# Attention and residual MLP on one core: MLP vectors scaled as rows and split on GpSimd, first head's q and k in halves

## The chip, the cores and the metric

The kernel runs on one core of one Trainium2 chip. The core has a matrix engine (TensorE, PE in the profile, with its weight loads as PEld), a vector engine (VectorE, DVE), a scalar engine (ScalarE, ACT), a general engine (GpSimd, POOL), an engine that mostly starts transfers (SyncE, SP), and 16 DMA engines. Each engine works through its own instructions in order and waits on semaphores for the others. The metric is the device time of one execution in microseconds (us).

## The reference

Block-sparse attention over 4 batches of 8 heads, 768 tokens and 64 dimensions, with a mask made of blocks of 32 tokens (neighbours, the first and the last block, and three drawn blocks for each row of blocks), then a residual MLP over 512 columns.

```python
scores = np.where(mask, scale * q @ k.T, -1e9)
x = softmax(scores) @ v                       # heads side by side: 4 x 768 x 512
a1 = alpha1 * x + beta1
tok = np.einsum('ts,bsd->btd', w_tok, a1)
u = x + lam * tok
a2 = alpha2 * u + beta2
ch = np.maximum(a2 @ w_ch1, 0.0) @ w_ch2
return (u + lam * ch).astype(np.float32)
```

`lam`, `alpha1` and `beta1` are vectors of 512. The product with `lam` is folded into other factors: `alpha1` and `beta1` are multiplied by it before they are used (tok comes out scaled), and `w_ch2` is multiplied by it in place (L453).

## The kernel before

**Tiling.** Heads are taken in pairs: 16 pairs `i`, four to a batch. Tokens are laid out as 6 slots of 128 (`NT = 6`). A unit is one pair, one half of its queries (`c`, 384 of them) and one step `j` of six; each unit computes two 128-key tiles of transposed scores for one head (`emit_qk`, L324: two matmuls into an `sp` buffer), one exponential of 128x768 on ACT (L332), and, two units later, six value products (`emit_pv`, L345). There are 192 units, one to a slot `s` of the main loop (L735). For the first pair the units are ordered so that steps 0 to 2 (the first head) of both query halves come first.

**Mask.** Each key tile carries 24 rows more (`kText[n][64:88]`) with the mask for the key's block, and the queries carry 24 indicator rows (`indq`), so that the mask is added by the score matmul. `mbs` (24x24) is worked out by DVE from `sampi` and `ms` (L195 to L210), spread into `kText[0]` in three parts of 256 columns (`emit_mask_part`, three copies each, L230), and copied to the other three buffers with `emit_mask_rows` (L236, on DVE).

**Start.** The first pair is loaded in float32 through SP's and ACT's DMA queues (`load_first`, L148, one DMA of 192 KB for a head and a tensor), later pairs by POOL's queue with a cast to 16 bits (`emit_load`, L111). `emit_lay` (L126) copies q and k side by side into `qk`; `emit_tps` transposes the six slots on PE (L267), and DVE copies the results into `kText` (L273) and `qText` (L276). `emit_warm` (L260) puts filler matmuls on PE; `spare` in `emit_qk` (L316) does the same inside the units. A copy of one element of v (`gate`, L187) stands on POOL ahead of the loads of pair 1.

**Vectors.** The three MLP vectors are loaded as 12 rows of 128 (`vrows`, L166). `emit_parts` (L400 to L404, DVE) splits each row into three bfloat16 parts; `emit_bcast(n)` (L409) multiplies a selection matrix (`pick`, L172) with them on PE, which puts vector `n` on all 128 partitions; L418 copies lam out of PSUM, and L420 copies alpha1 and beta1, times lam. `emit_lam16` (L437) casts lam to bfloat16 for L453. `emit_a1pp` (L376, L377) on POOL uses the two products.

**MLP.** `emit_wtok_t` transposes w_tok (L468, copied by L469), `job_tok` multiplies it with `a1pp` (L485), `job_f1` and `job_f2` are the two dense products (L553, L572).

**Order.** It is written out by hand. `at(s, ...)` hangs functions into slot `s`; up to slot 54 they run at the slot's end, from slot `OPEN = 55` on before its value products, and there a queue of MLP jobs is poured in beside them. Engines execute in the order in which the program issues to them. Transfers on SP and ACT signal eight semaphores in rotation, so a DMA also waits for the one that used its semaphore before.

Of the kernel before, what the change touches and what calls it, by code (L numbers as in the profile page):

```python
# [20 lines left out]
S = 768  # L21
# [20 lines left out]
def kernel(  # L42
# [73 lines left out]
    def emit_lay(i, nm, w=slice(0, 2), copy=None):  # L116
        raw = raws[(i, nm)][:, w].rearrange("p w (o d) -> p w o d", d=D)
        if nm != "v" and i >= XP:
            dst = (qls if nm == "q" else kls)[i % 2][:, w, :, 0:D]
        elif nm == "v":  # L120
            dst = vexts[i % NVB][:, w, :, 0:D]
        else:
            if i not in qks:
                qks[i] = ap_.tile([P, 2, NT, 2, D], BF, name="qk", tag="qk", bufs=2)
            dst = qks[i][:, w, :, "qk".index(nm), :]
        (copy or nc.vector.tensor_copy)(out=dst, in_=raw)  # L126
# [20 lines left out]
    def load_first(nm, src, w, eng):  # L147
        eng.dma_start(  # L148
            raws[(0, nm)][:, w, :], src[0, w].rearrange("(p o) d -> p (o d)", o=NT)
        )  # L150

    load_first("q", q, 0, nc.sync)
    load_first("k", k, 0, nc.scalar)
# [3 lines left out]
    load_first("v", v, 0, nc.scalar)  # L157
    nc.sync.dma_start(qText[0][D : D + NBLK, :], indq_dr.ap())
    load_first("k", k, 1, nc.scalar)
# [4 lines left out]
    vrows = ptile([P, P], FP, "vrows")  # L164
    for n, src in enumerate((moe_lam, moe_alpha1, moe_beta1)):
# [19 lines left out]

    gate = ptile([P, 1], FP, "gate")
    nc.gpsimd.tensor_copy(out=gate[:], in_=raws[(0, "v")][:, 0, 0:1])  # L187
# [4 lines left out]
    emit_lay(0, "q", slice(0, 1))  # L192
    emit_lay(0, "k", slice(0, 1), nc.scalar.copy)
    rndf = ptile([P, NR], FP, "rndf")
    nc.vector.tensor_copy(out=rndf[0:NBLK, :], in_=sampi[0:NBLK, 0 : 2 * NR : 2])  # L195
    mbm = ptile([P, NBLK], FP, "mbm")
# [67 lines left out]
    def emit_tps(i, w):  # L264
        tps = mm_tile((P, NT, P), BF)
        for o in range(NT):
            nc.tensor.transpose(tps[:, o, :], qks[i][:, w, o], identb[:])  # L267
# [3 lines left out]
        qa = 0  # L271
# [108 lines left out]
    vbc = ptile([P, 3, DM], FP, "vbc")  # L380
    lam_bc, a1_bc, b1_bc = (vbc[:, n, :] for n in range(3))
# [16 lines left out]
    def emit_parts():  # L398
        r = slice(0, 12)
        nc.vector.tensor_copy(out=parts[r], in_=vrows[r])  # L400
        nc.vector.tensor_sub(out=rest[r], in0=vrows[r], in1=parts[r])
        nc.vector.tensor_copy(out=part[r], in_=rest[r])
        nc.vector.tensor_copy(out=parts[32:44], in_=rest[r])
        nc.vector.tensor_sub(out=parts[64:76], in0=rest[r], in1=part[r])  # L404

    def emit_bcast(n):
# [28 lines left out]

    def emit_lam16():
        nc.vector.tensor_copy(out=lam_bcb[:], in_=lam_bc)  # L437
# [237 lines left out]

    for s, n in ((0, 1), (1, 2), (2, 1)):
# [136 lines left out]
```

## Time and profile before

| | |
|---|---|
| median of 3 runs | 324.46 us (324.38 to 324.64) |
| time of the profiled execution | 324.88 us |
| span of the profiled execution | 323.1 us |
| PE busy | 315.6 us, 98% of the span |
| ACT busy | 223.2 us, 69% |
| DVE busy | 140.0 us, 43% |
| POOL busy | 99.0 us, 31% |
| exponentials (L332) | 192 of 901 ns |
| first dense products (L553) | 512 matmuls of 325 ns |
| first score matmul | at 6.19 us |
| first exponential | at 7.03 us |
| first matmul of L553 | at 57.68 us |

The span runs from the first instruction to the last; the time of a run also holds what lies around it (1.78 us for the profiled execution). A line of an engine's timeline gives the start, the busy time, the engine, the line and operation, what it writes and reads, and in square brackets how long the engine stood idle before it and who released it. An entry with x8 stands for eight instructions merged. Busy times of matmuls hold a drain that overlaps the next one.

### The profile page before, as it was taken

Reading aid. Unit: us, or ns where it says so; the run is one execution under the profiler, and the core shown is the slowest. Engines: PE = TensorE matmul, PEld = TensorE weight load, DVE = VectorE, ACT = ScalarE, POOL = GpSimd, SP = SyncE. Lnnn points to the kernel's source line nnn. Section 1 sums busy time; section 2 is a strip of 40 time slices with the busy share of each in tenths; the row PEclk is TensorE's granted clock in tenths of the full one; section 3 lists DMA queues with packets and bytes.
Section 4 is the critical chain, followed back from the end, with each engine's and each line's share of the span. In section 5 each row is a group of like instructions: output and inputs, shape, how many; then the busy total and the mean of one; then the engine's idle time right before and its main releaser. Section 6 shows DMA issues by size and latency. Waiting matters only on the chain.

```text
span 323.1 us, 7663 instructions
## 1 busy us (share of the span) xinstructions
PE 315.6 (98%) x3216; PEld 205.7 (64%) x3216; DVE 140.0 (43%) x289; ACT 223.2 (69%) x328; POOL 99.0 (31%) x128
## 2 busy tenths in 40 slices
PE   8889999999999999999999999999999999999996
PEld 3667878667675766676665756676665756555543
DVE  4889988557343345331534444242332434000011
ACT  4889998998878776878768675678877740553310
POOL 7566746443434411132525402142222200000000
PEclk9999999999999999999999999999999999999999
DMA  6999996969392976091665966097430011000012
GB/s 168 197 191 164 143 156 110 165 114 140 57 177 54 169 120 131 32 172 27 127 103 96 138 106 128 34 155 74 108 52 32 15 46 65 32 34 32 32 43 89
DMA packets 61898, 32.56 MB, mean 101 GB/s; under 512 B 42000, under 2 KB 58756, under 8 KB 61736
## 3 DMA queue, kind: packets, MB, share of 16 engines
q0 software_dynamic: 16608, 14.22, 31.2%
q1 hardware_dynamic: 44680, 17.23, 25.2%
q10 hardware_dynamic: 576, 0.62, 0.7%
q8 instruction: 25, 0.41, 0.5%
q14 instruction: 9, 0.07, 0.1%
HBM read 29.97 MB, written 6.29 MB: 112 GB/s over the span
## 4 chain that ended last, share of the span: by engine, by line
PE 90%; DVE 7%; POOL 1%; issue 1%; ACT 1%; DVEq 0%; POOLq 0%
PE mm L553 26%; PE mm L572 25%; PE sp L324 16%; PE mm L485 10%; PE op L345 9%; PE op L260 1%; PE mm L592 1%; DVE qTs L276 1%; DVE wtokT L469 1%; DVE kTs L273 1%; PE mm L267 1%; DVE qk L126 1%; DVE x_sb L362 1%; POOL a1pp L376 1%; POOL a1pp L377 1%
## 5 line engine op out<-in xcount | busy, mean ns | idle before, releaser
L332 ACT ACTIVATE eT<-sp,expb 128x768 f16<-128x768 f32 x192 | 170.4, 901 | 47.3 <-PE sp L324 44.6
L553 PE MATMUL mm<-uT,w1b 128*128 128x384 bf16 x512 | 100.1, 325 | 0.0
L324 PE MATMUL sp<-qTs,kTs 88*128 88x384 bf16 x384 | 95.5, 326 | 0.9 <-ACT eT L332 0.5
L572 PE MATMUL mm<-w2b,hts 128*128 128x512 bf16 x368 | 92.3, 379 | 0.0
L560 ACT ACTIVATE hts<-mm 128x384 bf16<-128x384 f32 x128 | 61.8, 488 | 35.4 <-PE mm L553 35.0
L376 POOL TENSOR_TENSOR a1pp<-x_sb,vbc 128x384 bf16<-128x384 f32 x28 | 28.3, 1009 | 150.7 <-DVE x_sb L362 150.7
L553 PEld LDWEIGHTS <-w1b 128*128 128x128 bf16 x512 | 49.3, 97 | 36.1 <-issue 0.9
L345 PEld LDWEIGHTS <-eT 128*128 128x128 f16 x1152 | 55.9, 97 | 21.9
L572 PEld LDWEIGHTS <-hts 128*128 128x128 bf16 x368 | 35.3, 97 | 33.9
L345 PE MATMUL op<-vext,eT 128*128 128x65 f16 x1008 | 53.8, 193 | 0.0
L581 DVE TENSOR_TENSOR ot<-x_sb,mm 128x512 f32<-128x512 f32 x23 | 15.8, 686 | 66.9 <-PE mm L572 66.9
L485 PE MATMUL mm<-a1pp,wtokT 128*128 128x128 bf16 x576 | 41.6, 219 | 0.9 <-DVE qTs L276 0.3
L485 PEld LDWEIGHTS <-wtokT 128*128 128x128 bf16 x576 | 35.6, 97 | 6.6 <-PE mm L345 0.4
L500 DVE TENSOR_TENSOR x_sb<-x_sb,mm 128x384 f32<-128x384 f32 x32 | 17.6, 550 | 49.3 <-PE mm L485 48.5
L324 PEld LDWEIGHTS <-kTs 88*128 88x128 bf16 x384 | 28.3, 98 | 6.9 <-issue 1.4
L377 POOL TENSOR_TENSOR a1pp<-a1pp,vbc 128x384 bf16<-128x384 bf16 x28 | 26.7, 952 | 2.2
L506 DVE CAST ubf<-x_sb 128x384 bf16<-128x384 f32 x32 | 17.7, 553 | 1.1
L360 DVE RECIPROCAL rcp<-op 128x6 f32<-128x6 f32 x28 | 5.3, 191 | 29.5 <-PE op L345 29.2
L362 DVE TENSOR_TENSOR x_sb<-op,rcp 128x384 f32<-128x384 f32 x28 | 15.6, 558 | 1.0
L539 DVE TENSOR_SCALAR uT<-uraw,ab2T 128x768 bf16<-128x768 bf16 x11 | 5.4, 493 | 16.8 <-DMA uraw<-ubf 16.8
L111 POOL DMA_DIRECT2D qr<-in_q_dram x15 | 11.4, 761 | 3.1 <-DVE qk L126 3.1
L111 POOL DMA_DIRECT2D kr<-in_k_dram x15 | 10.8, 721 | 0.9 <-DVE qk L126 0.9
(74 smaller groups left out, 147.4 us busy)
## 6 DMA issues: line engine op xcount, KB each, us to landing
out_dram<-ot SPq DMA_DIRECT2D x23, 256.0 KB
qr<-in_q_dram POOLq DMA_DIRECT2D x15, 192.0 KB, 4.6
kr<-in_k_dram POOLq DMA_DIRECT2D x15, 192.0 KB, 6.3
vr<-in_v_dram POOLq DMA_DIRECT2D x15, 192.0 KB, 6.8
w1b<-in_moe_w_ch_dram POOLq DMA_DIRECT2D x4, 512.0 KB, 6.4
w2b<-in_moe_w_ch_dram POOLq DMA_DIRECT2D x4, 512.0 KB, 6.7
hts<-in_moe_w_tok_dram POOLq DMA_DIRECT2D x1, 1152.0 KB, 11.2
kf<-in_k_dram ACTq DMA_DIRECT2D x2, 192.0 KB
```

The lines of the kernel that those rows point to most:

```text
L111: nc.gpsimd.dma_start(t[:], src[b, 2 * hp : 2 * hp + 2].rearrange("w (p o) d -> p w (o d)", o=NT))
L324: nc.tensor.matmul(sp[:, jj, 0:QC], kText[n][0 : D + NBLK, ts(2 * jp + jj, P)], qText[n][0 : D + NBLK, ts(c, QC)], start=True, stop=True,)
L332: nc.scalar.activation(eT[:], sp[:, :, 0:QC], AF.Exp, bias=expb[:], scale=SCALE)
L345: nc.tensor.matmul(op[:, w, o, :], eT[:, jj, ts(o, P)], vexts[i % NVB][:, w, 2 * jp + jj, :], start=(j == 0 and jj == 0 and o == 0), stop= ...
L362: nc.vector.tensor_tensor(out=x_sbs[b][:, ts(c, 3), cols].rearrange("p o (w d) -> p w o d", w=2), in0=op[:, :, :, 0:D], in1=rcp[:].unsquee ...
L376: eng.tensor_tensor(out=dst, in0=x_sbs[b][:, sl, cols], in1=bc[0], op=ALU.mult)
L377: eng.tensor_tensor(out=dst, in0=dst, in1=bc[1], op=ALU.add)
L485: nc.tensor.matmul(ps[:, o % 3, :], wtokT[:, os_, ts(o, P)], a1pps[i][:, os_, :], start=(os_ == 0 and o % 3 == 0), stop=(os_ == NT - 1 and ...
L506: nc.vector.tensor_copy(out=ubfs[i][:, sl, :], in_=x_sbs[b][:, sl, ts(hp, P)])
L553: nc.tensor.matmul(ps[:, 0:QC], w1b[:, dk, ts(n, P)], uTs[b][:, dk, ts(c, QC)], start=(dk == 0), stop=(dk == 3),)
L560: nc.scalar.activation(hts[(b, c)][:, n, :], ps[:, 0:QC], AF.Relu)
L572: nc.tensor.matmul(ps[:], ht[:, nk, ts(o % 3, P)], w2b[:, nk, :], start=(nk == 0), stop=(nk == NH - 1),)
```

## The change

Four things are changed.

1. The first head's q and k are loaded, cast and transposed in two halves of three slots. The first halves are both cast by DVE, of the second halves k by POOL and q by DVE. The first scores are issued between the two sets of transposes. One filler matmul less stands ahead of them. On the DMA queues, the second k half and the query indicators follow on ACT, and v and the second head's k move to SP. The gate copy is gone.
2. `lam` is loaded twice more, as rows beside alpha1 and beta1 (`lrows`, whose first four rows are ones). `emit_parts` runs on POOL, begins with the product of the rows, and is issued before the main loop, ahead of the load of w_tok. `emit_bcast` then only copies; alpha1 and beta1 go into slots 6 and 7, lam directly into its bfloat16 form in slot 61.
3. The mask rows of buffers 2 and 3 are copied by DMA from SP in slot 2 instead of by DVE in slots 9 and 11.
4. Some slots move: the casts and transposes of pair 3, one token job, and the two scalings of u.

```diff
-    load_first("q", q, 0, nc.sync)
-    load_first("k", k, 0, nc.scalar)
+    load_first("q", q, 0, nc.sync, 0)
+    load_first("k", k, 0, nc.scalar, 0)
     nc.sync.dma_start(sampi[0:NBLK, :], sampled_blocks.bitcast(I32))
     nc.scalar.dma_start(identb[:], ident_dr.ap())
     nc.sync.dma_start(ms[0:NBLK, :], ms_dr.ap())
-    load_first("v", v, 0, nc.scalar)
-    nc.sync.dma_start(qText[0][D : D + NBLK, :], indq_dr.ap())
-    load_first("k", k, 1, nc.scalar)
+    load_first("k", k, 0, nc.scalar, 1)
+    load_first("q", q, 0, nc.sync, 1)
+    nc.scalar.dma_start(qText[0][D : D + NBLK, :], indq_dr.ap())
+    load_first("v", v, 0, nc.sync)
+    load_first("k", k, 1, nc.sync)
     load_first("q", q, 1, nc.sync)
     load_first("v", v, 1, nc.sync)
...
+    lrows = ptile([P, P], FP, "lrows")
+    nc.gpsimd.memset(lrows[0:12], 1.0)
+    for n in (1, 2):
+        nc.sync.dma_start(
+            lrows[4 * n : 4 * n + 4, :], moe_lam.rearrange("(c d) -> c d", d=P)
+        )
...
-    gate = ptile([P, 1], FP, "gate")
-    nc.gpsimd.tensor_copy(out=gate[:], in_=raws[(0, "v")][:, 0, 0:1])
...
-    emit_lay(0, "q", slice(0, 1))
-    emit_lay(0, "k", slice(0, 1), nc.scalar.copy)
     rndf = ptile([P, NR], FP, "rndf")
     nc.vector.tensor_copy(out=rndf[0:NBLK, :], in_=sampi[0:NBLK, 0 : 2 * NR : 2])
+    for nm in "qk":
+        emit_lay(0, nm, slice(0, 1), o=slice(0, 3))
...
     cuts = [(0, 2 * P, QC), (2 * P, S, S)] if i == 0 else [(0, S, S)]
+    if part is not None:
+        cuts = [(0, QC, QC), (QC, S, S)][part : part + 1]
...
     def emit_parts():
-        r = slice(0, 12)
-        nc.vector.tensor_copy(out=parts[r], in_=vrows[r])
-        nc.vector.tensor_sub(out=rest[r], in0=vrows[r], in1=parts[r])
-        nc.vector.tensor_copy(out=part[r], in_=rest[r])
-        nc.vector.tensor_copy(out=parts[32:44], in_=rest[r])
-        nc.vector.tensor_sub(out=parts[64:76], in0=rest[r], in1=part[r])
+        r, eng = slice(0, 12), nc.gpsimd
+        eng.tensor_mul(out=vrows[r], in0=vrows[r], in1=lrows[r])
+        eng.tensor_copy(out=parts[r], in_=vrows[r])
+        eng.tensor_sub(out=rest[r], in0=vrows[r], in1=parts[r])
+        eng.tensor_copy(out=part[r], in_=rest[r])
+        eng.tensor_copy(out=parts[32:44], in_=rest[r])
+        eng.tensor_sub(out=parts[64:76], in0=rest[r], in1=part[r])
...
-        if n == 0:
-            nc.vector.tensor_copy(out=lam_bc, in_=ps[:])
-        else:
-            nc.vector.tensor_tensor(
-                out=vbc[:, n, :], in0=ps[:], in1=lam_bc, op=ALU.mult
-            )
+        nc.vector.tensor_copy(out=dst, in_=ps[:])
...
+    emit_mask_part(0, nc.scalar.copy)
+    emit_tps(0, 0, 0)
+    for nm, eng in (("k", nc.gpsimd), ("q", nc.vector)):
+        emit_lay(0, nm, slice(0, 1), eng.tensor_copy, o=slice(3, NT))
+    emit_mask_part(1, nc.scalar.copy)
+    emit_warm(1)
     emit_load(1)
-    emit_mask_part(0, nc.scalar.copy)
-    emit_mask_part(1, nc.scalar.copy)
-    emit_tps(0, 0)
-    emit_warm(2)
-    emit_mask_part(2, nc.vector.tensor_copy)
+    emit_parts()
     emit_wtk_load()
...
+    at(0, lambda: emit_tps(0, 0, 1))
+    at(0, lambda: emit_mask_part(2, nc.vector.tensor_copy))
...
-    at(4, emit_parts)
     at(5, lambda: emit_lay(0, "v", slice(1, 2)), emit_columns)
-    at(9, lambda: emit_mask_rows(2))
-    at(11, lambda: emit_mask_rows(3))
-    at(6, lambda: emit_bcast(0))
-    at(7, lambda: emit_bcast(1))
-    at(8, lambda: emit_bcast(2))
+    rows = slice(D, D + NBLK)
+    for i in (2, 3):
+        at(2, lambda i=i: nc.sync.dma_start(kText[i][rows, :], kText[0][rows, :]))
+    at(6, lambda: emit_bcast(1, a1_bc))
+    at(7, lambda: emit_bcast(2, b1_bc))
+    at(61, lambda: emit_bcast(0, lam_bcb[:]))
...
-    at(60, emit_lam16)
...
-        3: (20, 21, 28, 27, 32),
+        3: (23, 24, 29, 28, 32),
...
-    tok_at(0, (22, 24, 25, 26, 28, 29))
+    tok_at(0, (22, 24, 25, 26, 27, 29))
     at(30, lambda: emit_udma(0))
-    at(47, lambda: emit_uscale(0))
+    at(44, lambda: emit_uscale(0))
...
-    at(54, lambda: emit_uscale(1))
+    at(51, lambda: emit_uscale(1))
```

More of the change, by code (lines that the diff above doesn't have):

```diff
@@ L114, in emit_load, with emit_lay @@
             raws[(i, nm)] = t
-    def emit_lay(i, nm, w=slice(0, 2), copy=None):
-        raw = raws[(i, nm)][:, w].rearrange("p w (o d) -> p w o d", d=D)
+    def emit_lay(i, nm, w=slice(0, 2), copy=None, o=slice(0, NT)):
+        raw = raws[(i, nm)][:, w].rearrange("p w (o d) -> p w o d", d=D)[:, :, o]
         if nm != "v" and i >= XP:
@@ L124, in emit_lay @@
                 qks[i] = ap_.tile([P, 2, NT, 2, D], BF, name="qk", tag="qk", bufs=2)
-            dst = qks[i][:, w, :, "qk".index(nm), :]
+            dst = qks[i][:, w, o, "qk".index(nm), :]
         (copy or nc.vector.tensor_copy)(out=dst, in_=raw)
@@ L145, with load_first @@
     maskt = ptile([P, NT, NBLK], BF, "maskt")
-    def load_first(nm, src, w, eng):
+    def load_first(nm, src, w, eng, half=None):
+        cols = slice(0, NT * D) if half is None else ts(half, NT * D // 2)
         eng.dma_start(
-            raws[(0, nm)][:, w, :], src[0, w].rearrange("(p o) d -> p (o d)", o=NT)
-        )
-    load_first("q", q, 0, nc.sync)
-    load_first("k", k, 0, nc.scalar)
+            raws[(0, nm)][:, w, cols],
+            src[0, w].rearrange("(p o) d -> p (o d)", o=NT)[:, cols],
+        )
+    load_first("q", q, 0, nc.sync, 0)
+    load_first("k", k, 0, nc.scalar, 0)
     nc.sync.dma_start(sampi[0:NBLK, :], sampled_blocks.bitcast(I32))
@@ L262, with emit_tps @@
     emit_warm(8)
-    def emit_tps(i, w):
+    def emit_tps(i, w, part=None):
         tps = mm_tile((P, NT, P), BF)
-        for o in range(NT):
-            nc.tensor.transpose(tps[:, o, :], qks[i][:, w, o], identb[:])
         n = (2 * i + w) % NQB
         cuts = [(0, 2 * P, QC), (2 * P, S, S)] if i == 0 else [(0, S, S)]
-        qa = 0
+        if part is not None:
+            cuts = [(0, QC, QC), (QC, S, S)][part : part + 1]
+        qa = 0 if cuts[0][0] == 0 else QC
+        for o in range(qa // P, cuts[-1][2] // P):
+            nc.tensor.transpose(tps[:, o, :], qks[i][:, w, o], identb[:])
         for ka, kb, qb in cuts:
@@ L377, in emit_a1pp @@
         eng.tensor_tensor(out=dst, in0=dst, in1=bc[1], op=ALU.add)
-    vbc = ptile([P, 3, DM], FP, "vbc")
-    lam_bc, a1_bc, b1_bc = (vbc[:, n, :] for n in range(3))
+    vbc = ptile([P, 2, DM], FP, "vbc")
+    a1_bc, b1_bc = (vbc[:, n, :] for n in range(2))
     ab2 = ptile([P, P], FP, "ab2")
@@ L398, in emit_parts, with emit_bcast @@
     def emit_parts():
-        r = slice(0, 12)
-        nc.vector.tensor_copy(out=parts[r], in_=vrows[r])
-        nc.vector.tensor_sub(out=rest[r], in0=vrows[r], in1=parts[r])
-        nc.vector.tensor_copy(out=part[r], in_=rest[r])
-        nc.vector.tensor_copy(out=parts[32:44], in_=rest[r])
-        nc.vector.tensor_sub(out=parts[64:76], in0=rest[r], in1=part[r])
-    def emit_bcast(n):
+        r, eng = slice(0, 12), nc.gpsimd
[5 more added lines that the diff above has]
+        eng.tensor_sub(out=parts[64:76], in0=rest[r], in1=part[r])
+    def emit_bcast(n, dst):
         ps = mm_tile()
@@ L434, in emit_columns_use @@
         nc.vector.tensor_copy(out=ab2T[:], in_=tps[:])
-    def emit_lam16():
-        nc.vector.tensor_copy(out=lam_bcb[:], in_=lam_bc)
     def emit_w1_load(g):
```

## The prediction

> **What bounds the kernel now.** I read the page's shares first, then each engine in order of time, then what each wait waited for.
>
> ```profile
> span 323.1 us, 7663 instructions
> PE 315.6 (98%) x3216; PEld 205.7 (64%) x3216; DVE 140.0 (43%) x289; ACT 223.2 (69%) x328; POOL 99.0 (31%) x128
> ...
> ACT  4889998998878776878768675678877740553310
> ...
> L553 PE MATMUL mm<-uT,w1b 128*128 128x384 bf16 x512 | 100.1, 325 | 0.0
> ```
>
> TensorE (PE) is busy throughout, but before 58 us part of its work is filler (L260, L316). There ScalarE (ACT) is at 8 to 9 tenths: one exponential (L332) after another. From then on the dense products rule, and the first of them never waits (idle 0.0 on L553). So the program is an exp chain up to some 58 us and a fixed pile of PE work behind it: what the first part saves moves the end by as much. The exps, in order of time:
>
> ```profile
> 3.91 0.51 ACT L126 CAST qk<-kf 128x384 bf16<-128x384 f32 x1
> 5.30 1.08 ACT L230 COPY kTs<-mbs 24x96 bf16<-24x96 bf16 x6 [0.88 <-DVE mbs L210]
> 7.03 3.28 ACT L332 ACTIVATE eT<-sp,expb 128x768 f16<-128x768 f32 x4 [0.65 <-PE sp L324]
> 10.50 2.50 ACT L332 ACTIVATE eT<-sp,expb 128x768 f16<-128x768 f32 x3 [0.19 <-PE sp L324]
> 13.88 7.25 ACT L332 ACTIVATE eT<-sp,expb 128x768 f16<-128x768 f32 x8 [0.88 <-PE sp L324]
> 21.67 7.13 ACT L332 ACTIVATE eT<-sp,expb 128x768 f16<-128x768 f32 x8 [0.54 <-PE sp L324]
> 29.21 0.90 ACT L332 ACTIVATE eT<-sp,expb 128x768 f16<-128x768 f32 x1 [0.42 <-PE sp L324]
> 30.37 22.32 ACT L332 ACTIVATE eT<-sp,expb 128x768 f16<-128x768 f32 x26 [0.25 <-PE sp L324]
> 53.30 5.64 ACT L332 ACTIVATE eT<-sp,expb 128x768 f16<-128x768 f32 x6 [0.62 <-PE sp L324]
> ```
>
> Square brackets hold the idle time and who ended it. Besides the start at 7.03 us there are gaps of 0.88, 0.54, 0.42, 0.25 and 0.62. PE ends each, but was itself late for VectorE (DVE):
>
> ```profile
> 12.58 0.28 DVE L404 TENSOR_TENSOR parts<-rest,part 12x128 bf16<-12x128 f32 x1
> 13.01 0.38 PE L409 MATMUL mm<-parts,pick 96*128 96x128 bf16 x4 [0.64 <-DVE parts L404]
> ...
> 20.94 0.20 PE L433 MATMUL mm<-ident,ab 8*128 8x8 f32 x1 [0.81 <-DVE rcp L360]
> ...
> 28.28 0.51 PE L485 MATMUL mm<-a1pp,wtokT 128*128 128x128 bf16 x6 [0.30 <-DVE wtokT L469]
> ```
>
> **The start: halves.** Eight warm matmuls (L260) start at 1.19 and every 0.427 us, so PE is free at 4.60 whatever the data do; q and k land by 4.03 now (k's landing releases the ninth DMA, SP's second q, at 3.87). Half loads carry half the packets (1536 bytes take 65 ns, 256 take 18), so they land some 0.5 us sooner, and the DVE casts (half of L126's 0.36: 0.21 each) end near 4.1: under the warm matmuls. The gain is in the three transposes: six take from 4.58 to 5.22, 0.107 apart, so three save 0.32. The DVE copies of three slots, 0.35 each (the 64x384 row), end at 5.85; first scores 5.90 for 6.19, first exp near 6.74 for 7.03. ACT's mask copies (3 x 0.18) follow `mbs` at 4.9 and are ready at 5.45.
> It is given back at once. The second halves' transposes stand behind the first scores: 5.90 + 2 x 0.32 = 6.54 to 7.05; DVE's kT copy to 7.42; one score tile 0.17, drain 0.17 and 0.05 to ACT: second exp 7.83 (now 7.85). The last mask part (3 copies, 0.53) runs behind both copies, to 8.35, so third scores end at 8.88 and the third exp starts at 8.92 (now 8.67). PE has the fifth ready in time; it starts near 10.56 (now 10.50). This half of the change is worth nothing by itself.
>
> **Vectors on GpSimd (POOL).** DVE loses five small operations, 0.21+0.28+0.21+0.22+0.28 = 1.20 us, two mask-row copies (0.56+0.35, now SP DMAs) and one 0.69 us step of L420. POOL gets six operations on 12x128, which this trace does not show. A tensor-tensor lies between the 0.20 of a 128x128 memset and the 1.01 of L376 on 384 columns; interpolating from the 0.19 of the gate copy (one column), 0.45. A copy lies between 0.19 and the 0.43 of a 128x288 one: 0.30. With 0.07 between steps, 2.6 us (1.2 to 4.7). The kf half cast on POOL (0.19 to 0.5, I take 0.35) hides under the first scores, to 6.54.
> When can they start? SP waits before a ninth DMA for the first of the last eight:
>
> ```profile
> SPq L148 <- DMA kf<-in_k_dram: 1.4, 1, 1.4
> ...
> SPq L172 <- DMA qf<-in_q_dram: 0.4, 1, 0.4
> ```
>
> After the change v and second k are on SP too, and the three vrows stand behind them and two lrows: the beta row leaves when second k has landed (near 6.5) and its packets follow v's in the ring. In the landing records now, v's last part ends at 7.86 and beta at 8.57; I put beta at 9.0, parts done at 11.6. The picks (L172; the third landed 4.3 us after its issue at 7.38) come near 11.5. PE reaches the broadcast behind the value products of the fifth exp, at 12.40 with the rows above (now 12.36, when it begins to wait). So the wait goes, and exp 8 starts at 13.2 for 13.88: 0.65 gained. Behind the waiting POOL stand the w_tok load (issue 8.06 now, 11.7 then) and pair 2's loads. That is covered: the first w_tok packet moves in the trace at 11.5, behind pair 1, which now leaves 0.8 us sooner; 11.7 + 1.64 (pair 1's issue to first packet) + 5.4 (its bytes at 110 KB per half us) + 0.3 = 19.0 for 19.3 now, wanted at 20.6. Without that cover pair 2's q, wanted 1.3 us later, is late next.
> The queues otherwise: ACT still issues four DMAs ahead of its table load; its new fourth, the query indicator (L158), lands near 4.5 behind less data than now (5.30) and is wanted at 5.90. SP issues v, second k, q and v from 3.3 to 5.0, each released by one of the small first ones; DVE wants them at 8.4 to 11.6, and landing at 6 to 7.9 hides that. The mask-row DMAs wait on SP for DVE's last mask part (8.35), and the alpha2, beta2 loads behind them are wanted only at slot 14. The gate copy that held pair 1 back goes; the kf cast now stands in its place.
> In 21.67's gap DVE was late with pair 1's copies (its queue held a mask-row copy and the slowed 1.05 us vext copy): 0.35 of 0.54 goes. In 29.21's gap a pair 3 cast (0.92) stood ahead of the last wtokT copy; it moves three slots down: 0.3 of 0.42. The other two gaps I leave, between all gone (0.87) and doubled; the casts and scales shifted there move DVE work no PE row names.
>
> **Late cost.** The lam broadcast moves from slot 6 to 61, where PE is the bound: 4 x 0.055 = 0.22, and up to 0.3 more for a PSUM buffer held by a 0.68 copy; I take 0.3. The copy itself replaces a 1.13 us cast (L437) on a DVE that then idles.
>
> **Sum** against the execution's own 323.1 (its run took 324.88, 0.42 above the median): -0.65 - 0.35 - 0.30 + 0.30 = -1.0, a span of 322.1; on the median of 324.46, 323.5. Own range 322.5 to 323.9: all gaps gone (another 1.1) or half of the gain kept.
>
> **Rivals.** *The clock.* Rows:
>
> ```profile
> 6.19 0.80 PE L324 MATMUL sp<-qTs,kTs 88*128 88x384 bf16 x2
> 6.79 0.53 PE L260 MATMUL op<-warm 128*128 128x512 bf16 x1
> 7.15 0.49 PE L324 MATMUL sp<-qTs,kTs 88*128 88x384 bf16 x2
> ```
>
> A pair of score matmuls takes 0.80, then 0.49: PE doubles its pace near 7.1, while the granted clock reads 1.00 throughout. PE was idle 0.12 us in between; after the change it has one warm matmul less and idles from 5.35 to 5.90. If the idling put the doubling off by 2 to 3 us (the count so far took 5.9, from 1.19), the second to fourth scores and their warm matmuls would cost 0.5 to 0.9 more, at 0.32 and 0.427 each in place of half of that: about 324.2.
> The Trainium skill (TensorE: Matmul & The Clock Gate, Part 1: The HAM clock gate) says the full clock comes after a busy window of about 3.4 us, in windows that run freely; this trace agrees as far as it goes (1.19 to 3.67 was not enough, 3.67 to 7.08 was), and by that rule a half us of idle may cost a whole window.
> *The gaps come back.* PE's slots are 0.85 us, ACT's exps 0.86 to 0.89, so a removed wait may show up one step on: half the gain, 324.1.
> *The vectors come late*, the slower side: POOL is in order, and PE stands at the broadcast until its sixth operation ends; past 12.4 each us is a us. Slow operations (4.7) or landings as slow as indt's (issued 8.62, landed 19) put the end at 14.4: +2.0, and w_tok then lands at 21.8, still just in time: 325.5. From 14.0 on it decides the sign. For it: transfers issued at 7 to 8 us took 4 us and more. Against: those met w_tok's 9216-byte packets, which can't start before the vectors are done.
>
> **Numbers.** Forecast 0.48, clock 0.13, gaps back 0.20, late vectors 0.19. About 0.2% (0.65 us) is what a measurement of this kernel can tell from no change. Faster: 0.46 of the first and some of the second group, 0.48; slower: 0.17; the same: 0.35. The range reaches from the forecast's low end into the late vectors: 322.5 to 325.2.
>
> **What would show it.** Right: first exp near 6.75 and third near 8.9; no wait on `parts` at the first broadcast (L409's successor), exp 8 near 13.2; L433's wait under 0.3; the last wtokT copy not waited for. Wrong: PE idle at the broadcast with POOL as releaser; scores at 0.80 a pair after 7.2; w_tok awaited; PE waits for a buffer near slot 61.

## The result and the profile after

The changed kernel took 326.56 us (median of 7 runs, 326.1 to 328.97) beside 324.56 us for the kernel before on the same chip (7 runs, 324.38 to 325.05): a ratio of 1.0068, with a 95% interval of 1.0049 to 1.0087. It is slower by 2.0 us, where 323.5 was forecast and 325.2 was the upper end of the range. The profiled execution took 326.56 us with a span of 324.8 us, against 324.88 and 323.1.

The seven runs are not alike in the clock that TensorE (PE) was granted. Its mean over the span was 1.000 in the profiled run and 0.990 to 0.995 in the other six; of the 97 runs of the kernel before beside the experiments, three had 0.995 and took 326.23 to 326.36 us, and all the others had 0.999 or 1.000. In the profiles below the clock falls to 0.50 in stretches of 3.4 us or a multiple, and one such stretch in 325 us makes a mean of 0.995. So most executions of the changed kernel had PE at half its clock for a while, which the profiled one did not. What follows is the account of the profiled one; where the others lost their time is not shown.

The timeline of ACT in the changed kernel (columns as before; L342 is the exponential, L334 the scores):

```profile
6.45 6.21 ACT L342 ACTIVATE eT<-sp,expb 128x768 f16<-128x768 f32 x7 [0.23 <-PE sp L334]
13.97 7.83 ACT L342 ACTIVATE eT<-sp,expb 128x768 f16<-128x768 f32 x9 [1.32 <-PE sp L334]
23.29 28.36 ACT L342 ACTIVATE eT<-sp,expb 128x768 f16<-128x768 f32 x33 [1.49 <-PE sp L334]
53.10 0.90 ACT L342 ACTIVATE eT<-sp,expb 128x768 f16<-128x768 f32 x1 [1.46 <-PE sp L334]
54.67 5.76 ACT L342 ACTIVATE eT<-sp,expb 128x768 f16<-128x768 f32 x6 [0.67 <-PE sp L334]
```

The exps start 0.58 us earlier than before, and the small gaps near 29 and 30 us are gone (33 exps follow one another). But there are three gaps of 1.3 to 1.5 us: ahead of the 8th, the 17th and the 50th exp. Who was late at the first two, on PE and then on POOL:

```profile
13.11 0.38 PE L421 MATMUL mm<-parts,pick 96*128 96x128 bf16 x4 [1.07 <-POOL parts L416]
...
22.33 0.54 PE L472 MATMUL mm<-identb,hts 128*128 128x128 bf16 x6 [1.36 <-DMA hts<-in_moe_w_tok_dram]
```

```profile
10.42 0.45 POOL L411 TENSOR_TENSOR vrows<-vrows,lrows 12x128 f32<-12x128 f32 x1 [3.16 <-DMA vrows<-in_moe_beta_dram]
...
12.63 0.42 POOL L416 TENSOR_TENSOR parts<-rest,part 12x128 bf16<-12x128 f32 x1
13.00 0.62 POOL L466 DMA_DIRECT2D hts<-in_moe_w_tok_dram  x1
```

POOL stood idle for 3.16 us until the beta row landed, PE then waited for POOL's last step, and the load of the token weights (`hts<-in_moe_w_tok_dram`, 1152 KB), behind those steps on POOL, left at 13.00 for 8.06 before. Its weights landed at 22.3, and PE waited for them too. At the third gap it is DVE:

```profile
46.89 0.36 DVE L126 COPY qk<-qr 128x768 bf16<-128x768 bf16 x1 [1.55 <-DMA qr<-in_q_dram]
...
49.77 0.47 DVE L543 TENSOR_SCALAR uT<-uraw,ab2T 128x768 bf16<-128x768 bf16 x1
50.16 1.08 DVE L126 COPY vext<-vr 128x768 f16<-128x768 f16 x1
51.16 0.54 DVE L504 TENSOR_TENSOR x_sb<-x_sb,mm 128x384 f32<-128x384 f32 x1
```

In the kernel before:

```profile
45.45 0.35 DVE L126 COPY qk<-qr 128x768 bf16<-128x768 bf16 x1
...
48.55 0.40 DVE L126 COPY vext<-vr 128x768 f16<-128x768 f16 x1
49.77 0.55 DVE L500 TENSOR_TENSOR x_sb<-x_sb,mm 128x384 f32<-128x384 f32 x1 [0.82 <-POOL a1pp L377]
```

The fifth pair's q came 1.4 us later, though POOL issued it at the same time (39.21 for 39.25), and ahead of the second x_sb now stand one of the moved scalings of u (0.47) and a vext copy that takes 1.08 for 0.40. PE's transposes of `ubf`, and behind them the scores, waited for that x_sb (51.16 for 49.77).

The start of each exponential in the traces, taken as differences (us), says what each stretch lost. The 192nd exp starts 1.56 us later than before, and the columns add up to that (the span is 1.66 us longer, the median 2.0):

| | to the 8th | 8th to 17th | 17th to 25th | 25th to 49th | 49th to 52nd | 52nd to 61st | 61st to 101st | 101st to 192nd |
|---|---|---|---|---|---|---|---|---|
| before | 13.88 | 8.83 | 7.66 | 20.57 | 3.24 | 11.29 | 55.29 | 139.19 |
| after | 13.97 | 9.32 | 6.89 | 20.57 | 4.75 | 11.31 | 55.51 | 139.19 |
| difference | +0.09 | +0.49 | -0.77 | 0 | +1.51 | +0.02 | +0.22 | 0 |

### The profile page after: what moved, and what is told of

It is laid out like the page before. It is cut to its first block, busy times and chain, and to the rows that moved or that the text cites. A ratio compares the mean times of both kernels' runs of the same rounds, so it can differ in the third digit from the quotient of the medians.

```text
span 324.8 us, 7636 instructions
## 1 busy us (share of the span) xinstructions
PE 313.0 (96%) x3183; PEld 205.3 (63%) x3215; DVE 136.3 (42%) x283; ACT 222.8 (69%) x327; POOL 101.4 (31%) x135
## 4 chain that ended last, share of the span: by engine, by line
PE 85%; DMA 8%; DVE 3%; POOL 2%; issue 1%; SPq 0%; POOLq 0%; DVEq 0%
PE mm L557 26%; PE mm L576 24%; PE sp L334 15%; PE op L355 8%; PE mm L489 8%; DMA hts<-in_moe_w_tok_dram 3%; DMA kr<-in_k_dram 2%; DMA kf<-in_k_dram 2%; PE mm L596 1%; DMA vrows<-in_moe_beta_dram 1%; PE mm L472 1%; DVE x_sb L504 1%; DVE ubf L510 1%; DVE kTs L283 1%; PE mm L519 0%
## 5 line engine op out<-in xcount | busy, mean ns | idle before, releaser
L342 ACT ACTIVATE eT<-sp,expb 128x768 f16<-128x768 f32 x192 | 170.4, 901 | 49.1 <-PE sp L334 45.9
L334 PE MATMUL sp<-qTs,kTs 88*128 88x384 bf16 x384 | 95.4, 326 | 1.6 <-DVE qTs L286 0.7
L576 PE MATMUL mm<-w2b,hts 128*128 128x512 bf16 x336 | 86.3, 379 | 1.7
L334 PEld LDWEIGHTS <-kTs 88*128 88x128 bf16 x384 | 28.3, 98 | 7.2 <-ACT kTs L238 0.9
L111 POOL DMA_DIRECT2D vr<-in_v_dram x15 | 10.8, 720 | 0.0
```

The lines of the kernel that those rows point to most:

```text
L111: nc.gpsimd.dma_start(t[:], src[b, 2 * hp : 2 * hp + 2].rearrange("w (p o) d -> p w (o d)", o=NT))
L334: nc.tensor.matmul(sp[:, jj, 0:QC], kText[n][0 : D + NBLK, ts(2 * jp + jj, P)], qText[n][0 : D + NBLK, ts(c, QC)], start=True, stop=True,)
L342: nc.scalar.activation(eT[:], sp[:, :, 0:QC], AF.Exp, bias=expb[:], scale=SCALE)
L576: nc.tensor.matmul(ps[:], ht[:, nk, ts(o % 3, P)], w2b[:, nk, :], start=(nk == 0), stop=(nk == NH - 1),)
```

## The experiments

All runs in one table; the kernel before took 324.57 to 324.60 (medians) beside them. "Least" and "most" are the range of the runs. The kernels with only 4 runs spread over 1.6 to 4.3 us, so small differences between them are not told.

| run | median (runs, least to most) | ratio, 95% interval |
|---|---|---|
| wtok_first | 330.47 (4, 329.11 to 331.91) | 1.0170, 1.0129 to 1.0210 |
| halves_only | 326.79 (10, 324.83 to 328.88) | 1.0063, 1.0035 to 1.0092 |
| vectors_only | 324.94 (10, 324.26 to 327.84) | 1.0011, 0.9989 to 1.0033 |
| rows_early | 327.21 (10, 325.32 to 329.38) | 1.0069, 1.0037 to 1.0101 |
| picks_early | 326.29 (4, 326.04 to 327.75) | 1.0063, 1.0040 to 1.0085 |
| halves_gate | 325.22 (10, 324.85 to 325.82) | 1.0019, 1.0010 to 1.0029 |
| halves_picks | 329.02 (4, 327.75 to 329.69) | 1.0133, 1.0109 to 1.0156 |
| vectors_best | 328.13 (4, 327.00 to 328.64) | 1.0106, 1.0081 to 1.0130 |
| gate_back | 326.58 (4, 325.82 to 328.89) | 1.0074, 1.0046 to 1.0102 |
| pick_small | 327.54 (4, 326.35 to 330.66) | 1.0107, 1.0069 to 1.0145 |
| gate_pick_small | 324.85 (10, 324.40 to 326.86) | 1.0013, 0.9996 to 1.0029 |
| order_best | 329.18 (6, 327.66 to 330.56) | 1.0145, 1.0118 to 1.0171 |
| before_pick_small | 324.78 (10, 324.55 to 325.18) | 1.0000, 0.9987 to 1.0013 |
| halves_gate_small | 324.85 (10, 324.40 to 326.41) | 1.0003, 0.9986 to 1.0019 |
| vectors_pick_small | 325.99 (10, 325.16 to 327.42) | 1.0038, 1.0019 to 1.0057 |
| gate_small_wtok | 329.80 (4, 328.74 to 330.54) | 1.0147, 1.0112 to 1.0182 |
| gate_small_slots16 | 325.11 (11, 324.69 to 326.06) | 1.0017, 1.0009 to 1.0026 |
| gate_small_slots17 | 326.90 (6, 326.07 to 327.61) | 1.0068, 1.0054 to 1.0082 |

### The token weights ahead of the vectors, and each half of the change alone

The first theory was that POOL's order is the loss: the vectors stand ahead of the token weights. The edit that undoes this order:

```diff
-    emit_parts()
     emit_wtk_load()
+    emit_parts()
```

> Theory (GpSimd's queue): the load of w_tok stands behind GpSimd's 3.16 us wait for the beta row and 2.63 us of vector steps, is issued at 13.0 and lands at 22.3, which makes the gap of 1.49 us before the 17th exp; the backlog it leaves on the DMA engines also makes the gap of 1.46 us before the 50th. With w_tok issued first (near 7.3) both fall under 0.8 us, while the gap of 1.32 us before the 8th exp stays or grows to some 2: 324.3 to 325.5. Rival (slots): the third gap comes from the scalings of u and the casts moved to other slots; then only the second gap goes and the third stays at 1.4 or so: 325.0 to 325.5.

It cost 3.9 us more. The table of waits (who, for what, us in total, times, longest) of this run:

```profile
PE mm L421 <- DMA pick<-pick_c: 5.6, 1, 5.6
...
POOL vrows L411 <- DMA vrows<-in_moe_beta_dram: 3.9, 1, 3.9
```

The gap ahead of the 17th exp went, as that theory has it, and the one ahead of the 50th fell from 1.46 to 0.28 (with everything 5.4 us later by then, so this doesn't settle what makes it). But PE stood 5.6 us for the selection (`pick`, three transfers of 36 KB on SP's queue): the token weights' 9216-byte packets were now on the same 16 DMA engines. The next run is the kernel before with the first head in halves, loads reordered and the gate copy taken out, and the vectors left on VectorE:

```diff
-    gate = ptile([P, 1], FP, "gate")
-    nc.gpsimd.tensor_copy(out=gate[:], in_=raws[(0, "v")][:, 0, 0:1])
...
+    for nm in "qk":
+        emit_lay(0, nm, slice(0, 1), o=slice(0, 3))
```

> The kernel before with the halves alone. Theory (GpSimd's queue): the halves are nearly worth nothing; first exp 6.5 to 6.8, w_tok issued near 7.3, no gap above 0.9: 323.8 to 324.8. Rival (halves): the start itself, with v and second k behind each other on SP, delays what follows: 325.2 or more.

And the rest of the change on the start of the kernel before, gate copy included; its edit against the changed kernel is the undoing of the first part of the change:

```diff
-    load_first("q", q, 0, nc.sync, 0)
-    load_first("k", k, 0, nc.scalar, 0)
+    load_first("q", q, 0, nc.sync)
+    load_first("k", k, 0, nc.scalar)
...
+    gate = ptile([P, 1], FP, "gate")
+    nc.gpsimd.tensor_copy(out=gate[:], in_=raws[(0, "v")][:, 0, 0:1])
```

> The changed kernel with the start of the kernel before. Theory (GpSimd's queue): the beta row is issued near 6.5 as before and lands near 9, so w_tok is issued near 12 instead of 13.0 and lands at 20.5 to 21.5: the loss stays, somewhat smaller, 325.0 to 326.3. Rival (halves): without them the loss is gone, 323.3 to 324.3.

The halves alone, which I had priced at nothing, cost 2.2 us; the vectors alone cost nothing that can be told (324.94, below the 325.0 to 326.3 of the theory). In the halves' run the vectors are still on VectorE, and yet the broadcast waits:

```profile
14.83 7.25 ACT L336 ACTIVATE eT<-sp,expb 128x768 f16<-128x768 f32 x8 [1.97 <-PE sp L328]
22.61 7.13 ACT L336 ACTIVATE eT<-sp,expb 128x768 f16<-128x768 f32 x8 [0.53 <-PE sp L328]
```

```profile
PE mm L413 <- DMA pick<-pick_c: 1.7, 1, 1.7
```

The gap ahead of the 8th exp went from 0.88 to 1.97, and the releaser is the selection, whose last part landed at 13.83. The token weights left POOL at 6.98 for 8.06, and their first packet moved at 10.76 for 11.69. So the late thing is the small transfers, not POOL's arithmetic. Without the gate copy POOL's queue starts a us sooner and takes the engines from them. That can be undone alone:

```diff
+    gate = ptile([P, 1], FP, "gate")
+    nc.gpsimd.tensor_copy(out=gate[:], in_=raws[(0, "v")][:, 0, 0:1])
     emit_load(1)
```

> The halves alone, with GpSimd's copy of one element of v put back ahead of the loads of pair 1. Theory (picks): holding pair 1 and w_tok back by 0.8 to 1.5 us lets the picks through; the third lands near 12 and the gap of 1.97 before the 8th exp falls under 1: 324.3 to 325.5, spread under 2 us. Rival (order on SP): the picks are late because they are issued late, at 7.0 to 8.9; the gap stays above 1.5 and the median above 326.

325.22 for 326.79; no wait for the selection is left, and the 8th exp starts at 13.56, 0.32 earlier than before. One copy of a single element (0.19 us) on POOL, which waits for the first v, is worth 1.6 us here. Some of the 1.6 is clock: three of the ten runs without the copy, the slowest (327.98 to 328.88), have a mean of 0.990 to 0.994, and all ten with it 0.999 or 1.000.

### The small transfers moved forward on SP

If the rows and the selection are late because four 192 KB loads stand ahead of them on SP, they can go first: the rows right behind the second half of q, or rows and selection ahead of the second head's v (on the changed kernel; on the halves alone; and on the vectors alone with the token weights first). The edit of picks_early, shortened:

```diff
     load_first("q", q, 1, nc.sync)
+    vrows = ptile([P, P], FP, "vrows")
...
+    pick = ptile([P, 12, P], BF, "pick")
...
     load_first("v", v, 1, nc.sync)
     nc.sync.dma_start(qText[1][D : D + NBLK, :], indq_dr.ap())
-    vrows = ptile([P, P], FP, "vrows")
...
-    pick = ptile([P, 12, P], BF, "pick")
```

> The changed kernel with the five row loads moved on SP to right behind the second q half. Theory (GpSimd's queue): the rows land near 6, GpSimd's steps run from 7.3 to 9.9, nothing waits at the first broadcast, and w_tok is issued near 9.9 and lands near 19: the 8th exp near 12.8, the 17th near 20.8, 322.6 to 323.8. Rival (slots): the third gap stays at 1.4: 324.0 to 324.6. Rival (GpSimd too slow): the steps slow down beside VectorE and the gap before the 8th exp stays above 1: 325 or more.

> The changed kernel with the row and pick loads issued on SP ahead of second v. Theory (picks): with the halves, four loads of 192 KB stand on SP ahead of the rows and picks, which then meet the loads of pair 1 and the 9216-byte packets of w_tok; PE's wait at the first broadcast is theirs, and so is the spread of the times. Ahead of second v the picks land before 10.5 and the rows near 8, so w_tok is issued near 11 for 13.0: gap before the 8th exp under 0.7 (1.32 in the changed kernel), w_tok awaited by less than 0.5, 323.5 to 325.0 and runs within 1.5 us of each other. Rival (GpSimd's queue alone): the rows make it, the picks do not matter; the same gain, but the runs spread as before.

> The halves alone, with the row and pick loads issued on SP ahead of second v. Theory (picks): they land before 10.5, PE waits for VectorE's parts at most, as in the kernel before: 323.8 to 324.7, spread under 1.5 us. Rival (halves): the start itself or VectorE's longer list at the start costs it: still above 325.5.

> The vectors on GpSimd with the start of the kernel before, rows and picks ahead of second v on SP, w_tok loaded ahead of GpSimd's steps. Theory (picks, and w_tok behind GpSimd's steps): nothing waits at the first broadcast (vectors_only: 1.02 before the 8th exp) nor for w_tok (0.86 before the 17th): 322.6 to 323.8, faster than the kernel before. Rival: w_tok's packets, moving earlier, delay the second head's v, the indicators and pair 1 instead, and a new wait takes their place: 324.3 or more.

None helped. The waits that took the place, in that order of runs:

```profile
DVE qk L126 <- DMA qf<-in_q_dram: 2.0, 1, 2.0
```

```profile
PE sp L334 <- DMA qTs<-indq_c: 2.8, 1, 2.8
```

```profile
PE sp L328 <- DMA qTs<-indq_c: 3.2, 1, 3.2
```

```profile
PE sp L331 <- DMA qTs<-indq_c: 3.2, 1, 3.2
```

With the rows first the second head's q is late (landed at 11.07); with rows and selection first it is the second head's indicator rows, 36 KB more on the same queue. Whatever is last on SP when POOL's loads get moving pays. In all four profiles the clock is at 0.50 for 3.4 or 6.8 us during or after that wait, which adds to the loss.

### Gate and size, one at a time and together

Two things can lighten the queue without moving anything: the gate copy back (the same two lines as above), and the selection made small, one 96x12 tile of 2.2 KB whose column is broadcast as the stationary operand, in place of three copies of 36 KB:

```diff
-    pick = ptile([P, 12, P], BF, "pick")
-    nc.gpsimd.memset(pick[:], 0.0)
-    for m in range(3):
-        nc.sync.dma_start(
-            pick[32 * m : 32 * m + 12],
-            pick_dr.ap().rearrange("r (n d) -> r n d", d=P),
-        )
+    pick = ptile([P, 12], BF, "pick")
+    nc.sync.dma_start(pick[0:96, :], pick_dr.ap())
...
-                pick[0:96, 4 * n + c, :],
+                pick[0:96, 4 * n + c : 4 * n + c + 1].broadcast_to([96, P]),
```

> The changed kernel with the gate copy put back on GpSimd ahead of the loads of pair 1 (behind the kf cast). Theory (the missing gate): as with the halves alone (326.79 without, 325.22 with), holding pair 1 until first v has landed lets rows and picks through: the beta row lands before 9.6 instead of 10.2, the gap before the 8th exp falls from 1.32 to under 0.8: 324.6 to 325.8, spread under 1.5 us. Rival (w_tok): pair 1 and w_tok only get later, w_tok is awaited still longer than 1.49 us: 326.3 or more.

> The changed kernel with the selection as a 96x12 tile in one small DMA, its column broadcast as the matmul's weights, in place of three DMAs of 36 KB and a memset. Theory (picks): their part of the wait goes, and with it most of the spread; the first broadcast then waits for GpSimd's parts alone, which end near 12.9: gap before the 8th exp 0.9 to 1.2, w_tok still awaited by 1.2 or more: 325.3 to 326.3, spread under 2 us. Rival (vectors): nothing changes, since parts and not picks come last: 326.3 to 326.8 with the old spread.

> Both: the gate back and the small selection. Theory: the two add up; what is left is w_tok behind GpSimd's steps (0.7 to 1.5 us) and the parts: 324.2 to 325.3. Rival: as gate_back within 0.3.

Neither alone recovers anything that can be told (326.58 and 327.54 for 326.56), both together recover nearly all (324.85). In pick_small the wait for the token weights was followed by 3.4 us at a clock of 0.50 (23.78 to 27.19), and the stretch from the 17th to the 25th exp took 8.33 us for 6.89. The waits say why. With the gate alone:

```profile
POOL vrows L411 <- DMA vrows<-in_moe_beta_dram: 1.6, 1, 1.6
...
PE mm L421 <- DMA pick<-pick_c: 1.3, 1, 1.3
```

With the small selection alone:

```profile
POOL vrows L408 <- DMA vrows<-in_moe_beta_dram: 3.8, 1, 3.8
...
PE mm L418 <- POOL parts L413: 1.4, 1, 1.4
```

With both, on POOL and on ACT:

```profile
8.91 0.60 POOL L408 TENSOR_TENSOR vrows<-vrows,lrows 12x128 f32<-12x128 f32 x1
...
11.14 0.42 POOL L413 TENSOR_TENSOR parts<-rest,part 12x128 bf16<-12x128 f32 x1
11.51 0.62 POOL L463 DMA_DIRECT2D hts<-in_moe_w_tok_dram  x1
```

```profile
8.81 12.16 ACT L339 ACTIVATE eT<-sp,expb 128x768 f16<-128x768 f32 x14 [0.28 <-PE sp L331]
22.28 28.35 ACT L339 ACTIVATE eT<-sp,expb 128x768 f16<-128x768 f32 x33 [1.30 <-PE sp L331]
```

There are two late things in a row. With the gate alone the large selection is still late, with the small selection alone the beta row is; either one holds PE at the same broadcast. With both, POOL's steps wait for no row, the last of them ends at 11.56, no gap over 0.28 is left between the first exp and the 17th, and the 8th starts at 13.14. What stays is 1.30 us ahead of the 17th: the token weights. How the landings stand to POOL's queue (us, from the records of transfers and landings of the profiled executions):

| | first packet of pair 1 | the rows' landings in the order of issue | beta |
|---|---|---|---|
| before | 7.37 | 8.21, 8.39, 8.57 | 8.57 |
| after | 6.84 | 8.06, 8.84, 9.02, 9.53, 10.21 | 10.21 |
| pick_small | 6.98 | 9.38, 9.56, 10.02, 10.44, 11.03 | 11.03 |
| gate_back | 7.93 | 8.57, 8.75, 8.93, 9.11, 10.00 | 10.00 |
| gate_pick_small | 8.04 | 7.99, 8.17, 8.35, 8.52, 8.70 | 8.70 |

Each row transfer is 2 KB. Where few packets of pair 1 have moved yet (before, gate_pick_small) they land 0.18 apart; once its 768-byte packets (79 ns each) move, mostly 0.4 to 0.9 apart (twice 0.18), and gate_back's last row shows the change of pace within one run. The Trainium skill (DMA: Bandwidth & Descriptors, Queues, rings and completion order) says that each DMA engine goes round the queues that have work and drains one queue's whole packet, some 9 to 17 descriptors, before it turns to the next; by that a small transfer costs a turn of the other queue, and a row's 0.4 to 0.9 us, 5 to 11 of the 79 ns records, agrees in order of size.

Is the small selection a gain by itself, and what are the vectors worth once arrivals are in order? Three runs: the small selection on the kernel before, on halves with gate, and on the vectors alone.

> The kernel before with only the selection made small: one 96x12 tile in one transfer in place of three of 36 KB each and a cleared 128x1536 tile, a column of it broadcast as the stationary operand. Theory (small transfers on the hardware queues share the engines packet by packet with the big loads, and the three selections were on the path only after the change): in the kernel before, the broadcasts waited for the parts on VectorE (0.6 us) and not for the selection, so this alone gains little at the first broadcast: 324.0 to 324.6, gaps of 0.79 and 0.54 us as before. Rival (the small selection is itself the whole cure, because 108 KB fewer pass ahead of pair 1 and of the token weights): 323.5 or less.

> The halves with the gate copy and the small selection, the vectors still on VectorE with twelve broadcasts: the version with gate and small selection less the vectors' part of the change. It tells what the move of the vectors to GpSimd and the rows are worth once everything has arrived in time. Theory (once arrival is in order the vectors' part takes 0.65 us off the wait ahead of the 8th exponential and gives it back at the 17th, since GpSimd issues the token weights only behind it): no gap at the 17th above 0.6, one of 0.7 ahead of the 8th, 324.5 to 325.2, that is the same as the version with both (324.85). Rival (the vectors' part is what costs): 323.8 or less.

> The vectors' part alone on the start of before, with the small selection. Theory: with the vectors alone PE waited 0.8 us for the selection ahead of the 8th exponential; that wait goes, and what is left is the 0.8 us for the token weights, issued at 11.6: 324.0 to 324.6. Rival (a shorter transfer only lets another one be late): a new wait of 1 us or more in the first 14 us, 325 or more.

On the kernel before it does nothing: 1.0000. Halves with gate and small selection, without the vectors' part, take 324.85, the same as with it, with gaps of 0.79 and 0.53 ahead of the 8th and the 16th exp, as expected. On the vectors alone PE's wait for the selection goes (gap of 0.48 ahead of the 8th exp for 1.02), but POOL waits 1.6 us for beta, the token weights come later (gap of 1.52 for 0.86), and 325.99 is 1.4 above the forecast's end: there the rival, that another transfer is late instead, has it. By stretches:

| | to the 8th | 8th to 17th | 17th to 25th | 49th to 52nd | 61st to 101st |
|---|---|---|---|---|---|
| halves_only | 14.83 | 8.83 | 7.65 | 3.24 | 55.29 |
| halves_gate | 13.56 | 8.93 | 7.66 | 3.24 | 55.29 |
| vectors_only | 13.48 | 8.69 | 6.89 | 3.78 | 55.56 |
| gate_pick_small | 13.14 | 9.14 | 6.88 | 3.84 | 55.51 |

In vectors_only and gate_pick_small the vectors' part and its slots change the last three columns by nearly the same, with either start: -0.77, +0.54 to 0.60, +0.22 to 0.27, together about nothing. With the halves the third gap is what it was (3.24).

### The token weights earlier, or their use later

With gate and small selection the weights leave POOL at 11.51 and are 1.2 us late. They can go ahead of the vector steps (the edit of wtok_first), or the six transposes that use them can go one or two slots down. The first of these was tried with the start of the kernel before, and with gate and halves:

> The vectors on GpSimd with the start of the kernel before (gate included), the small selection, and w_tok's load ahead of GpSimd's steps. Theory (late small transfers, and w_tok behind GpSimd's steps): rows land near 9.2, parts end near 12, selection near 9.5, w_tok near 19: gaps under 0.4 before the 8th and the 17th exp (vectors_only: 1.02 and 0.86): 322.8 to 323.9, faster than the kernel before by 0.2 to 0.5%. Rival: the mask rows and indicators of pair 1, now transfers behind w_tok's packets, take the place of the old wait: 324.5 or more.

> The version with gate and small selection, and the token weights issued ahead of GpSimd's vector steps instead of behind them. In that version there was no wait ahead of the 8th exponential, and 1.3 us ahead of the 17th for the token weights (issued 11.51, gap against 0.54 before). Theory (what is late is set by order of arrival: with the gate the rows and the selection have landed by 8.9, before the weights' packets move): the gap ahead of the 17th falls to 0.5 or less and the vectors end 0.6 us later, at 12.2, with a gap of 0.3 at most ahead of the 8th: 323.6 to 324.3, under before. Rival (the weights' 9216-byte packets go ahead of whatever is still on the hardware queues, the second head's indicators or the alpha and beta columns): a new wait of 2 us or more, 327 or more, as with the weights first and the large selection (330.47).

With wtok_first they are the slowest of the study. PE's timeline with gate, halves, small selection and the weights first:

```profile
13.06 0.39 PE L418 MATMUL mm<-parts,pick 96*128 96x128 bf16 x4
...
18.96 0.80 PE L331 MATMUL sp<-qTs,kTs 88*128 88x384 bf16 x2 [2.43 <-issue]
```

The broadcast is in time. But the scores at 18.96 are the first of pair 1, and they need the mask rows that the change copies by DMA (`kTs<-kTs`, 36 KB each, issued on SP at 9.58). The first of these copies has its last landing at 18.87; in gate_pick_small at 13.78. The profile names no releaser ("issue"); that it is this copy is read from the landing, 0.09 us ahead of the matmul. Again the weights' 9216-byte packets are ahead of a small transfer.

```diff
-        at(15 + o, lambda o=o: emit_wtok_t(o))
+        at(16 + o, lambda o=o: emit_wtok_t(o))
```

> The version with gate and small selection, with the six transposes of the token weights one slot later each (slots 16 to 21 for 15 to 20; the first token job stays in slot 22). In that version the 17th exponential starts at 22.28 after a gap of 1.30 us, because PE's first transpose waits 1.2 us for the token weights and the scores stand behind it. Theory (the late weights are all that is left of the loss, and they are 0.4 us too late for slot 16): the 17th exponential starts near 21.2 with no gap, one of about 0.4 us stands ahead of the 18th, and 0.85 us is kept to the end: 323.7 to 324.2. Rival (an arrival or a unit later on takes it back, such as the fifth pair's q): the early gap goes as said, the third gap near 50 us grows by as much, 324.5 to 325.

> The same with the transposes in slots 17 to 21, the last two both in slot 21, so that the first needs the token weights 0.9 us later again. Theory: no wait for the weights at all, 0.4 us under the version with slots 16 to 21 if nothing else ends there, 323.4 to 324.0; the two transposes in one slot and the token job behind them cost 0.35 us of PE near 26 us. Rival (as above, a later wait takes it back): 324.5 to 325, with the third gap larger.

With slots 16 to 21 the 17th exp starts at 21.07 with no gap, as expected, but then this, in DVE's timeline of that run:

```profile
23.16 0.57 DVE L128 COPY qk<-qr 128x768 bf16<-128x768 bf16 x1 [3.23 <-DMA qr<-in_q_dram]
23.65 0.54 DVE L470 COPY wtokT<-mm 128x768 bf16<-128x768 bf16 x1
```

The q of pair 2 is queued behind the weights on POOL's queue, and its cast now stands ahead of the weights' first copy on DVE; so the late queue is paid for at the next place, in three gaps of 1.17, 1.12 and 0.54 us. With 17 it is one of 3.05. 325.11 and 326.90: the rival, that a later wait takes the gain back, holds, though not at the place it named (the stretch from the 49th to the 52nd exp is 3.34 and 3.35, shorter than in gate_pick_small). Part of it is that beta landed late again (POOL waited 1.3 and 1.8 us), with the same start as gate_pick_small: so which transfer is last differs between executions of the same start.

No kernel of the study is faster than the kernel before beyond doubt. gate_pick_small's 192nd exp starts 0.36 us earlier than in the before's profile, yet its median is 0.3 above.

## Why the prediction was wrong, point by point

**The start.** Forecast: first, third and fifth exp at 6.74, 8.92 and 10.56, worth nothing. Measured: 6.45, 8.41 and 10.16. The gain of 0.34 at the fifth comes from PE's pace, in this timeline of the changed kernel:

```profile
4.58 0.38 PE L281 MATMUL mm<-identb,qk 128*128 128x128 bf16 x3
4.84 0.38 PE L268 MATMUL op<-warm 128*128 128x512 bf16 x1
5.92 0.48 PE L334 MATMUL sp<-qTs,kTs 88*128 88x384 bf16 x2 [0.71 <-DVE qTs L286]
```

A warm matmul takes 0.38 already at 4.84, a pair of scores 0.48; in the kernel before the first pair took 0.80 at 6.19. The profile's records of the granted clock begin just where the pace doubles, at 4.67 here and at 7.08 in the kernel before. But that moment differs between executions: it lies between 3.98 and 7.08 in the six profiles with the start of the kernel before, and between 4.42 and 7.11 in those with the halves. So the 0.34 is luck of the two profiled executions, and the clock rival is not borne out: with the halves the moment never comes later than 7.11. Over all profiles the first exp starts at 6.50 to 7.21 with the old start and at 6.30 to 6.81 with the halves, the fifth at 9.97 to 10.68 and at 10.01 to 10.88 (13.10 in rows_early, where q was late): "worth nothing" was right. One reading was not: the half loads do not carry half the packets, but as many of half the size (768 bytes, 36 ns, for 1536 and 65), and the first k half landed 0.85 us sooner (3.01 for 3.86), not 0.5.

**"The gate copy that held pair 1 back goes"** was told and priced at nothing: this is the step that failed first. It held pair 1's packets back. In the halves alone their first moves at 7.66 with the copy and at 7.02 without, beta lands at 9.17 and 10.01, the last part of the selection at 12.28 and 13.83, and the copy is worth 1.6 us. In the changed kernel with the small selection it is worth 2.7 (327.54 to 324.85), in the changed kernel by itself nothing that can be told, since the large selection is then late.

**"I put beta at 9.0, parts done at 11.6. The picks come near 11.5."** The six steps took 2.63 us for the 2.6 estimated. But beta landed at 10.21, the last step ended at 13.05, and the 8th exp came at 13.97 for the 13.2 forecast: +0.09 in place of -0.65. That the mechanism was right shows in gate_pick_small: with beta at 8.70 and the steps done at 11.56 the 8th exp is at 13.14.

**The argument against the late vectors** was that slow transfers "met w_tok's 9216-byte packets, which can't start before the vectors are done". True of those, but pair 1's 768-byte packets did it. The rival's point of decision (steps done at 14.0) was not reached, so it was right in its mechanism and sign and not in its place: at the vectors the forecast gain went (0.74), and the net loss came behind them.

**"That is covered"**, of the token weights: issued at 11.7, landed at 19.0, wanted at 20.6. They left at 13.00 and landed at 22.3: the stretch from the 8th to the 17th exp +0.49 for -0.35. Even issued at 11.51 (gate_pick_small) they landed at 21.3; from the first packet to there it took 8.4 us (12.85 to 21.27), and 8.0 in the changed kernel, for the 5.7 that I took. The kernel before had already needed 7.6 (11.69 to 19.30), so its own trace could have shown it: 7.6 in place of 5.7 makes 20.9, past the 20.6. So the term is mis-sized by more than 2 us even with the vectors in time.

**The gap at 29.21**: -0.30 forecast, -0.77 measured, both small gaps gone: right, and larger. **The late broadcast of lam**: +0.30 forecast, +0.22 measured.

**"The other two gaps I leave."** The last of them grew by 1.51. Some 0.6 of it is in every kernel that holds the moved slots and the early gains (vectors_only, gate_pick_small, vectors_pick_small), none in those with the halves alone; which of the moved steps does it was not tried by itself, the scaling of u that moved from slot 54 to 51 stands in front of the late x_sb. The rest goes with the fifth pair's q, which landed 1.5 us later (46.87 for 45.37) though issued at the same time. Its first packet moved 0.6 us later (43.14 for 42.53), behind a load of `w1b` on the same queue that landed at 43.84 for 42.77. Right ahead of it stands a DMA transpose of `ubf`, and 58 of q's 256 packets took 0.2 to 1.6 us each there (0.08 is usual); in the kernel before 29 did, with 1.2 to 1.4. Why it was longer stays open.

The sum goes from -1.0 to the 1.56 of the table: 0.74 by late arrivals at the 8th exp, 0.84 by the weights, 1.51 by the third gap, less 0.47 and 0.08 of gains and costs that were better than forecast (the rest is rounding). That is for the profiled executions; between the medians it is 2.0, and a PE at half its clock in the middle of the program, as in the other runs, was no term of the sum.

## What to carry to other kernels

A copy that seems to do nothing on the queue that issues loads may be what lets the small, urgent transfers land first; before it is removed, list what is in flight on the other queues and when each is wanted. Price a small transfer by what moves on the DMA engines when its turn comes, not by its bytes, and make it small or early enough to land before the bulk starts; moving it up a queue only changes who is late. Work put on the engine that issues loads delays every load behind it, and a late queue is paid for again at each later place that waits for it.

## What the runs showed of the hardware

- A 2 KB transfer on SP's queue landed every 0.18 us with little beside it, and mostly every 0.4 to 0.9 us beside POOL's 768-byte packets. Beside the 9216-byte packets (0.7 us each) PE's wait for the 36 KB selections reached 5.6 us, and a 36 KB copy landed 5.1 us later (18.87 for 13.78).
- A stationary operand read as one column broadcast over 128 columns runs as fast as a stored one: the broadcast's matmuls took 217 to 222 ns in gate_pick_small, and 217 to 222 in the kernel before with the stored one.
- After some waits PE runs at half its pace for several us. The windows of gate_small_wtok (busy us and counts by engine, then the granted clock as the third number from the end, the DMA share and GB/s):

```profile
16.00:18.00 2.00, 0.53 (x11) 0.33 (x7) 1.24 (x4) 1.42 (x2) 0.84 (x1) 1.00 1.01 218
18.00:20.00 2.00, 1.04 (x10) 0.73 (x11) 0.00 (x0) 0.14 (x1) 1.76 (x3) 0.60 1.16 181
20.00:22.00 2.00, 2.00 (x21) 1.57 (x18) 1.11 (x2) 0.97 (x2) 0.00 (x0) 0.50 1.31 201
...
26.00:28.00 2.00, 2.00 (x22) 1.62 (x21) 1.34 (x4) 0.94 (x2) 0.41 (x1) 0.50 0.75 85
```

PE stood idle for 2.43 us, and the granted clock was 0.50 from 18.42 to 28.66 us, with scores at 0.80 a pair. So that wait came with a median 4.95 us above gate_pick_small's, twice its length. The same in the other profiles (us):

| run | PE idle | stretch at 0.50 |
|---|---|---|
| changed kernel | 1.07, 1.36 | none |
| vectors_pick_small | 1.39 | none |
| pick_small | 1.42, 1.53 | 3.4 behind the second |
| halves_only | 1.73 | none |
| rows_early | 1.91 | 3.4 |
| order_best | 2.69 | 6.8 |
| picks_early | 2.82 | 6.8 |
| halves_picks | 3.24 | 3.4 |
| vectors_best | 3.25 | 6.8 |
| wtok_first | 5.61 | 6.8 |

The stretches come in steps of 3.4 us, and the length of the wait alone decides neither whether one follows nor how long it is. In the kernel before a run with a mean clock of 0.995, as one stretch makes it, took 1.7 us more than the median. The Trainium skill (TensorE: Matmul & The Clock Gate, HAM oscillation — how this bites in real kernels) puts it at waits for a DMA of more than some 3.4 us, after which PE falls to half its clock and the transition is paid for again. These traces differ in the length: most of the waits that were followed by it were shorter, the shortest 1.53 us.
